# Splitting operations of an attention and feed-forward kernel in two, with a new order list

## The chip, the cores and the metric

The kernel runs on one core of one Trainium2 chip. The metric is the device time of one execution in microseconds. Where the text says TensorE, VectorE, ScalarE, GpSimdE and SyncE, the profile says PE (with PEld for its weight loads), DVE, ACT, POOL and SP.

## The reference

Inputs are q, k and v of 2 batches, 8 heads, 768 positions and 64 channels, and two pairs of weight matrices (512 x 2048 and 2048 x 512).

```
k_sum = max of k over blocks of 32 positions;  v_sum = mean of v over the same blocks
scores_l = q @ k.T / 8, kept where |i - j| < 16, else -1e9
scores_s = q @ k_sum.T / 8 + log(32)
a = softmax over [scores_l, scores_s];  x = a @ [v, v_sum]        # 1536 tokens x 512 channels
h = x @ w_in1;   x = (h * cos(h)) @ w_out1
h = x @ w_in2;   out = (h * clip(h + 3, 0, 6) / 6) @ w_out2
```

## The kernel before

**Attention** is cut into 12 units of 128 queries and all 8 heads. For a unit the keys are the 96 of a window for each half of the queries and the 24 block maxima, together 120 columns. `front(u)` (line 625) loads the queries, puts the mask into two PSUM banks (`masks`, a matmul, or from unit 7 on `seed`, a copy), adds the scores (`scores`), takes the row maxima (`largest`, line 694), the exponentials with their sums (`power`, line 703, one activation for each head), the inverse of the sums, and multiplies with it (`scaled`, line 714). The index j in these operations is the half of the heads, one PSUM bank each. Units 0 and 1 are cut into two groups by heads in another way (`halves`) and so have two of each of these operations already. `back(u)` (line 717) transposes the result on TensorE (`flip`, twice) into bank b, copies it out (`flipped`), multiplies it with the window's values and block means (`weighted`, in 64 small matmuls) and splits the sum into two fp32r parts (`x hi`, `x lo`). The block means of v come from matmuls (`means`, line 580) and are copied by `put_v` (line 589) into rows 96 to 119 of a tile `vcats`: for buffer 0 from PSUM (`put v`, four copies), for buffer 1 from buffer 0 (`put v on`, one copy). This is done once for each batch, so twice.

**Feed-forward.** The weights are loaded, taken apart and put together again as fp32 (`carry`, `rebias`, `shift`, `join`) and split into high and low parts (`hi`, `lo`). Three fp32r products stand for one fp32 product. `first` is the first layer's products (two matmuls in each operation), `turns`, `rest`, `cosine` and `gate` its activation, `second` the second layer's products. In the first stage feed-forward works on 256 tokens at a time, that is on two units, and is woven into the attention of later units; later it works on 512 tokens, in part by block products (`mm1_set`).

**The order.** Every operation is one call of `G.op`, which gives it a number, the engines that may run it and what it reads and writes. Nothing is scheduled by the program: the string `ORDER` (line 39) has one word for each operation, in the order of issue, as `p20+1` or `a1`. The letter is the engine (p TensorE, a ScalarE, v VectorE, g GpSimdE, s SyncE), the number is the operation, and each engine runs its own words in this order, waiting for what they read. `+n` has `fill(n)` (line 1043) issue n matmuls of zeros, 128x512, behind the operation. Ahead of the first feed-forward operation they write into bank d1, which holds nothing yet. Line 1047 is theirs. A word `we` or `ws` loads a table on ScalarE ahead of its use. Loads are issued by SyncE alone, in the order of its words.

The functions that the diff touches:

Of the kernel before, what the change touches and what calls it, by code (L numbers as in the profile page):

```python
# [22 lines left out]
P = 128  # L23
WIN = 16
BLK = 32
# [7 lines left out]
def wstart(w, seq):  # L33
# [6 lines left out]
    s8 p6 s7 s19 s10 s36 a1 g2 s11 v13 a4 a5 s62 s9 v12 p20+1 v0 p21 p37+1 v22 s277 p38+1 v15 a23 s64 v16 a24 v39 p68+2  # L40
    s284 v40 v14 s63 a41 p28+1 v17 p29 v25 s53 a279 v26 v278 p45 g27 a3 v30 p46 a103 s291 v31 p76+2 v47 a32 s84 v280 v48
    s65 p69 v120 p70 a286 v281 p54+2 a49 v33 v287 v42 p55 s66 v34 g35 s67 a77 g282 p85 v56 s101 a293 p78 g283 s80 p86
    v79 a57 s97 a58 v43 v18 v294 p71+3 v292 v50 v87 g295 p72+1 v51 p73 s118 g44 a88 v74 p102 a89 s305 g52 p104 g296 p93
    v59 p81 v60 v105 g61 p95+4 a82 s114 v94 s138 a106 v96 g75 s136 p110+2 v83 v285 p98 v90 v111 g288 s135 v91 p112 a99
    v297 p119 a307 p359 v113 p360 a306 p361 v107 v308 p121 s131 a289 v108 g309 v100 p115 s137 v122 g92 a310 p362 s145
    a116 v142 p347 p348 a123 p363 p349 v117 s298 g311 p371 p364 v140 p350 p127 p372 g109 v128 p351 p352 p373 v139 p129
    a353 s179 p374 a130 p375 v124 g290 v354 p376 a365 v125 p132 a377 v141 s158 g147 v366 p146 s175 v133 g143 a355 p148
    v134 a367 v356 a300 p154 v378 g357 v368 p383 a155 g126 p384 v149 p385 a379 p399 p156 a299 p400 v157 p401 s312 p386
    g358 p402 s188 p159 v301 s162 v380 g302 a150 s189 p403 s190 v160 p404 p417 p418 g303 v161 p387 p419 g369 p395 v304
    p171 s191 g181 a405 p420 v172 p421 a163 p388 s193 p422 g164 v406 p173 s192 a314 p397 g144 v174 p398 g381 a389 p412  # L50
    v151 a423 v315 p176 v313 v152 v390 g153 p165 v177 s223 a407 s206 a391 v178 p396 s319 p411 g316 s210 v166 p413 p194
    p195 p196 p197 v392 g317 p198 we a167 v424 p199 v408 g370 p435 p436 v200 p451 g393 s227 p437 p452 g382 p438 p439
    g318 p440 p415 p453 a441 s326 v180 p414 p416 g212 p202 p429 v442 g394 p182 v203 a425 a443 v409 v426 p204 s244 v183
    g427 p454 p455 g229 p431 p432 v205 g410 we a184 p469 p470 v168 p207 v434 v169 g170 p449 v208 p471 p450 v209 p464
    a211 p466 p430 v320 g201 p219 v444 a321 p456 v220 p213 a433 g428 s333 a328 s240 v322 p221 a457 v214 g323 p472 a222
    p447 p473 a327 p224 v185 v445 a215 v186 s340 v329 g187 v458 p474 v225 s257 p448 p463 p465 v226 p467 p481 g324 p236
    a475 g330 v228 p487 a237 p488 p489 p490 p238 v216 g446 v476 p482 v217 v239 g325 p230 a459 v485 a477 p241 g246 v231
    g218 p468 s265 v242 p491 we a232 p492 p499 v478 p483 v243 p484 g479 v460 p500 p253 v461 p503 v254 p504 p515 p517
    a245 v233 p505 v234 p255 v480 g235 p521 a493 p247 a256 a486 p258 a335 v248 g331 a342 g462 p522 s273 a259 v494 p506
    g332 p507 a249 p501 v260 p519 p502 v336 p516 v334 p261 p518 g337 s556 v262 p533 p523 p524 p263 v250 p508 v251 v264  # L60
# [183 lines left out]
def attention_two_ffn(  # L244
# [344 lines left out]
    def put_v(b, i):  # L589
        mb = "b" if b else "e"  # L590
        every = [("vcs", i, c) for c in range(P // BLK)]
        if i == 0:
            CC = DM // (P // BLK)

            def put(e):
                for c in range(P // BLK):
                    hs = slice(c * CC // D, (c + 1) * CC // D)
                    copy(e, vcat[0][WK:KC, :, hs, :], bank[mb][BLK * c:BLK * c + NB, 0:CC].rearrange(
# [772 lines left out]
```

## Time and profile before

| | us |
|---|---|
| median of 3 runs | 568.65 (568.09 to 569.66) |
| time of the profiled execution | 568.47 |
| its span, first to last instruction | 566.7 |
| TensorE busy | 560.5 |
| VectorE busy | 462.1 |
| ScalarE busy | 340.1 |
| GpSimdE busy | 226.4 |

The profiled execution is one run with the profiler on; its span leaves out what lies around the first and last instruction. A matmul's start is measured and its end modelled, and matmuls overlap in the array, so for TensorE the distance from one start to the next tells more than the duration of one.

### The profile page before, as it was taken

To read this page: it belongs to the slowest core of one execution; us is meant where nothing else is said; L and a number is where in the kernel's file an instruction comes from. 1 tells how busy PE (TensorE), PEld (TensorE's weight loads), DVE (VectorE), ACT (ScalarE), POOL (GpSimd) and SP (SyncE) were. 2 spreads that over 40 slices of the span, in tenths; PEclk is the share of its full clock that TensorE was granted. 3 is DMA by queue.
4 is the path that set the end of the run, shared out by engine and by line. 5 is a ranking of instruction groups with operands and counts; after the bars stand their busy time and mean duration, and the time that the engine had idled before them with its cause. 6 is when DMAs were issued, how large, how long until landed. Compare 5 with 4: busy or idle time off the path is not lost.

```text
span 566.7 us, 9919 instructions
## 1 busy us (share of the span) xinstructions
PE 560.5 (99%) x3741; PEld 478.2 (84%) x3741; DVE 462.1 (82%) x857; ACT 340.1 (60%) x726; POOL 226.4 (40%) x222
## 2 busy tenths in 40 slices
PE   9999999999999999999999999999999999999996
PEld 6789999888888888888889888888888889888885
DVE  6898979888989988979899998777878597766653
ACT  5989995757547786666658677645653443322130
POOL 3788875646533214435253552041132303122111
PEclk9999999999999999999999999999999999999999
DMA  8989532323012211232200222223213220200103
GB/s 318 274 249 294 167 96 99 113 84 102 0 39 74 76 38 38 80 124 95 74 2 1 75 74 75 75 93 132 74 30 119 75 75 1 75 1 1 43 33 149
DMA packets 17232, 51.49 MB, mean 91 GB/s; under 512 B 1952, under 2 KB 2464, under 8 KB 17184
## 3 DMA queue, kind: packets, MB, share of 16 engines
q1 hardware_dynamic: 17184, 50.86, 27.2%
q8 instruction: 29, 0.48, 0.3%
q14 instruction: 19, 0.16, 0.1%
HBM read 47.71 MB, written 3.15 MB: 90 GB/s over the span
## 4 chain that ended last, share of the span: by engine, by line
PE 95%; DMA 2%; POOL 1%; SPq 1%; issue 0%; DVE 0%; ACT 0%; DVEq 0%; POOLq 0%
PE bank_a L1077 24%; PE bank_d L894 16%; PE bank_b L1077 11%; PE bank_c L1077 11%; PE bank_e L894 9%; PE bank_c L894 9%; PE bank_d L946 4%; PE bank_e L946 2%; PE bank_c L946 1%; PE bank_b L736 1%; DMA total<-in_vw_dram 1%; PE bank_b L752 1%; PE bank_c L668 1%; PE bank_d L1047 1%; DMA vcats<-in_vw_dram 1%; PE bank_d L530 1%
## 5 line engine op out<-in xcount | busy, mean ns | idle before, releaser
L517 ACT ACTIVATE cv_t<-raw 128x512 f32<-128x512 f32 x64 | 42.9, 677 | 20.4 <-DVE plo L463 7.5
L522 POOL TENSOR_TENSOR cv_y<-cv_t,cv_y 128x512 int32<-128x512 int32 x25 | 34.4, 1381 | 39.7 <-ACT cv_y L508 18.9
L446 ACT CAST ghi<-hs 128x512 fp32r<-128x512 f32 x43 | 26.5, 617 | 21.6 <-DVE hs L1033 12.8
L1037 DVE TENSOR_TENSOR glo<-hs,ghi 128x512 fp32r<-128x512 f32 x46 | 34.8, 759 | 3.4 <-ACT ghi L446 2.6
L508 ACT ACTIVATE cv_y<-raw 128x512 int32<-128x512 uint32 x47 | 30.9, 668 | 8.5 <-POOL plo L463 4.2
L1037 POOL TENSOR_TENSOR glo<-ch_c,ghi 128x512 fp32r<-128x512 f32 x11 | 15.3, 1390 | 50.7 <-ACT ghi L446 42.4
L520 DVE TENSOR_SCALAR cv_t<-cv_t 128x512 int32<-128x512 int32 x64 | 28.8, 452 | 4.7 <-ACT cv_t L517 4.3
L463 POOL TENSOR_TENSOR plo<-cv_y,phi 128x512 fp32r<-128x512 f32 (+1 forms) x14 | 17.0, 1216 | 32.7 <-ACT phi L446 30.9
L522 DVE CUSTOM_DVE_ANT_0 cv_y<-cv_t,cv_y 128x1024 uint16<-128x1024 uint16 x39 | 27.2, 703 | 1.4 <-ACT cv_y L508 1.3
L714 POOL TENSOR_TENSOR es<-es,rs 128x960 f32<-128x960 f32 (+1 forms) x14 | 21.9, 1565 | 15.5 <-ACT es L706 10.6
L706 ACT ACTIVATE es<-bank_c,nmx 128x120 f32<-128x120 f32 x80 | 27.6, 376 | 0.1
L894 PE MATMUL bank_d<-xhi,plo 128*128 128x256 f32 (+1 forms) x106 | 26.3, 329 | 0.0
L894 PE MATMUL bank_d<-xlo,phi 128*128 128x256 f32 (+1 forms) x106 | 26.2, 329 | 0.0
L894 PE MATMUL bank_d<-xhi,phi 128*128 128x256 f32 (+1 forms) x106 | 26.2, 328 | 0.0
L446 ACT CAST ghi<-ch_c 128x512 fp32r<-128x512 f32 x26 | 16.0, 616 | 12.5 <-DVE ch_c L1033 7.1
L910 DVE TENSOR_TENSOR ch_c<-bank_d,ch_c 128x256 f32<-128x256 f32 (+1 forms) x31 | 14.2, 461 | 10.4 <-PE bank_d L894 8.7
L1124 DVE SCALAR_TENSOR_TENSOR total<-bank_a,total 128x512 f32<-128x512 f32 x28 | 19.0, 685 | 3.3 <-PE bank_a L1077 3.3
L1077 PE MATMUL bank_a<-ghi,whi_out 128*128 128x512 f32 x60 | 21.3, 390 | 0.0
L1077 PE MATMUL bank_a<-ghi,wlo_out 128*128 128x512 f32 x60 | 21.3, 389 | 0.0
L1077 PE MATMUL bank_a<-glo,whi_out 128*128 128x512 f32 x60 | 21.2, 389 | 0.0
L1037 POOL TENSOR_TENSOR glo<-hs,ghi 128x512 fp32r<-128x512 f32 x7 | 10.2, 1457 | 27.5 <-DVE ghi L446 12.5
L894 PEld LDWEIGHTS bank_d<-xhi,phi 128*128 128x128 f32 x106 | 18.8, 189 | 2.8
(398 smaller groups left out, 1967.7 us busy)
## 6 DMA issues: line engine op xcount, KB each, us to landing
raw<-in_w_in_dram SPq DMA_DIRECT2D x32, 512.0 KB, 3.4
raw<-in_w_out_dram SPq DMA_DIRECT2D x32, 512.0 KB, 3.4
vcats<-in_vw_dram SPq DMA_DIRECT2D x12, 384.0 KB, 5.8
qt<-in_q_dram SPq DMA_DIRECT2D x12, 256.0 KB, 6.0
ktile<-in_kt_dram SPq DMA_DIRECT2D x7, 384.0 KB, 5.3
total<-in_vw_dram SPq DMA_DIRECT2D x8, 256.0 KB, 5.3
out_dram<-total SPq DMA_DIRECT2D x8, 256.0 KB, 2.1
vnat<-in_vw_dram SPq DMA_DIRECT2D x4, 256.0 KB, 4.8
```

The costliest lines, as they stand in the source:

```text
L446: nc.scalar.copy(o, i) if e == "ACT" else VEC[e].tensor_copy(o, i)
L508: nc.scalar.activation(y, low.bitcast(U32), AF.Copy, scale=2.0 ** -29)
L517: nc.scalar.activation(o, a, AF.Prelu, scale=2.0 ** -112, alpha=-2.0 ** 32)
L520: G.op("shift", {"DVE": dve(DM, 2)}, lambda e: nc.vector.tensor_scalar(t, t, 3, None, ALU.logical_shift_left), w=[tk], twice=True)
L522: G.op("join", {"POOL": pool(DM), "DVE": dve(DM)}, lambda e: VEC[e].tensor_tensor(y, t, y, ALU.add), r=[tk], w=[yk], twice=True)
L706: nc.scalar.activation(ef[:, j, hp], s4[j][:, hp, :], AF.Exp, bias=nmx[:, j, hp:hp + 1], scale=scale if direct else 1.0, accum_out=sm[:, j ...
L714: G.op("scaled", {"POOL": pool(2 * nz * KC, 1.25) - 0.07, "DVE": dve(2 * nz * KC)}, lambda e, ef=ef, rs=rs, nz=nz: VEC[e].tensor_tensor(ef ...
L894: nc.tensor.matmul(o, wt[i][:, A[a], kk * P:(kk + 1) * P], xt[:, kk, :], start=first and p + kk == 0, stop=p + kk == 3, skip_group_check=True)
L946: nc.tensor.matmul(h, w["in"][i][:, kk * P:(kk + 1) * P], x[blk][:, kk, c0:c1], start=p + kk == 0, stop=p == 2 and kk == NK - 1)
L1037: G.op("g lo", {"DVE": dve(N), "POOL": pool(N)}, lambda e: VEC[e].tensor_tensor(gbuf("lo", s)[:, 0:N], c(), gh().bitcast(F32), ALU.subtrac ...
L1077: nc.tensor.matmul(acc(s, i)[0], l, r, start=first, stop=end and p == 2 and (N == TOK or i % 2 == 1), skip_group_check=N < TOK)
L1124: G.op("sums", {"DVE": dve(TOK)}, lambda e: nc.vector.scalar_tensor_tensor(t(), a, 1.0 / 6.0 if m else 1.0, t(), ALU.mult, ALU.add), r=[ak ...
```

## The change

Four kinds of operation become two operations each, with the same instructions in them except where the text says otherwise:

- `largest` of units 4 to 11 and `power` of units 2 to 11: one operation for each bank j.
- `scaled` of units 2 to 11: one operation on each half of the heads. This was one instruction of 128x960 and is two of 128x480.
- `put v`: two copies in each operation instead of four in one.
- `put v on`: two copies of half the heads instead of one of all.

The keys on which the operations depend are made finer in the same way, so that a transpose of the first half waits for the first half's scaling alone. This adds 32 operations (2,579 to 2,611).

```
-            G.op("put v", {...}, put, r=[mb], w=every)
+            for cs in ((0, 1), (2, 3)):
+                G.op("put v", {...}, lambda e, cs=cs: put(e, cs), r=[mb], w=[every[c] for c in cs])
...
-            G.op("put v on", {...}, ..., r=[("vcs", 0, c) for c in range(P // BLK)], w=every, twice=True)
+            for half in range(2):
+                hs = slice(half * H // 2, (half + 1) * H // 2)
+                G.op("put v on", {...}, ..., r=[("vcs", 0, c) for c in (2 * half, 2 * half + 1)], w=every[2 * half:2 * half + 2], twice=True)
...
+            for js in (both,) if direct else ((0,), (1,)):
+                G.op("largest", {...}, ..., r=[spk[j] for j in js], w=key("max" if direct else "mx", js))
...
+            for js in (both,) if first else ((0,), (1,)):
+                G.op("power", {...}, ..., r=key("mx", js) + [spk[j] for j in js], w=key("e", js) + key("sm", js), table="exp")
...
+            for js in (both,) if first else ((0,), (1,)):
+                G.op("scaled", {...}, ..., r=key("rs", js), w=key("e", js), twice=True)
```

`ORDER` is written anew. From TensorE's word for `first#116` on, at about 100 us, the sequence of every engine is as before; the order ahead of it is changed. TensorE's words up to the first feed-forward operation, with names for numbers (the count behind # is that of the operation of this kind in the program):

```
before: wake masks#0+1 scores#0 masks#2+1 scores#2+1 means#0+2 masks#1+1 scores#1 masks#3 scores#3 flip#0+2 means#1 means#2
        masks#4+2 scores#4 masks#5 flip#1 scores#5 means#3+3 means#4+1 means#5 masks#6 scores#6 flip#2 weighted#0 flip#3+4
        flip#4+2 weighted#1 flip#5 masks#7 first#6
after:  wake masks#0+1 scores#0 masks#2+4 scores#2+2 means#0+1 masks#1 scores#1+3 masks#3 scores#3+2 flip#0+2 masks#4 scores#4
        flip#2 means#1 means#2 masks#5 scores#5 flip#1+6 means#3 means#4+1 means#5 masks#6 scores#6 flip#3+2 weighted#0+3
        flip#4+4 weighted#1 masks#7 flip#5 first#6
```

The zero matmuls in them are 20 before and 31 after. Between the first feed-forward operation and the last weighted sum stand 124 operations `first` and `second` before and 114 after; the rest follow it.

74 operations change their engine, all in this part. The larger groups: `flipped` 8 from VectorE to ScalarE and 4 back; `x hi` 4 from ScalarE to VectorE; `carry` 4 to ScalarE and 3 to VectorE; `join` and `lo` 8 from GpSimdE to VectorE and 4 back; `g hi` and `g lo` 6 from GpSimdE to VectorE and 5 back; `hi` 3 from ScalarE to GpSimdE; `seed` 2 from ScalarE to VectorE and 1 back; for the second batch half of `put v` from VectorE to ScalarE and half of `put v on` from GpSimdE to VectorE; `scaled` of one group of unit 0 and one half of the last unit from GpSimdE to VectorE.

GpSimdE's order has the first half of `put v on` ahead of the scaling of unit 2, where the whole stood behind it, and the copies of keys (`window`, `put k`) of units 6 and 7 further ahead. SyncE's order has the queries of unit 2 in the tenth place instead of the 13th and those of unit 5 ahead of the window load of unit 1 instead of behind it; the other loads of keys, values and weights change places with their neighbours. On ScalarE `x hi` of units 0 and 1 is gone from between the exponentials.

## Rows read from the trace of the kernel before

**Rows 1.** The page, its first line and part 1 (busy us, share, instructions).

```profile
span 566.7 us, 9919 instructions
...
PE 560.5 (99%) x3741; PEld 478.2 (84%) x3741; DVE 462.1 (82%) x857; ACT 340.1 (60%) x726; POOL 226.4 (40%) x222
```

**Rows 2.** The timeline of TensorE: start us, us, what, matmuls merged (x).

```profile
29.04 0.64 PE L946 MATMUL bank_d<-xhi,phi 128*128 128x256 f32 x4
29.52 0.40 PE L946 MATMUL bank_d<-xhi,plo 128*128 128x256 f32 x2
...
103.76 0.84 PE L946 MATMUL bank_e<-xhi,plo 128*128 128x512 f32 x3
104.44 1.07 PE L946 MATMUL bank_e<-xlo,phi 128*128 128x512 f32 x4
```

**Rows 3.** The table of windows; its second line names the columns.

```profile
core 0: us, PE busy (x) PEld busy (x) DVE busy (x) ACT busy (x) POOL busy (x), PEclk, DMA share, GB/s
1.05:29.04 27.99, 27.99 (x471) 20.63 (x472) 21.20 (x56) 21.22 (x97) 15.63 (x32) 1.00 0.95 306
29.04:98.00 68.96, 68.38 (x971) 63.23 (x971) 60.56 (x125) 60.53 (x183) 52.52 (x54) 1.00 0.58 183
...
40.00:60.00 20.00, 19.79 (x291) 18.29 (x290) 17.19 (x37) 19.06 (x55) 17.05 (x22) 1.00 0.76 251
60.00:80.00 20.00, 20.00 (x314) 18.64 (x314) 16.44 (x38) 19.57 (x69) 15.91 (x15) 1.00 0.42 121
```

**Rows 4.** The table of waits of TensorE, whole run.

```profile
PE bank_d L530 <- DVE zero L378: 1.1, 1, 1.1
PE bank_c L668 <- POOL kcat L623: 0.4, 1, 0.4
PE bank_b L582 <- DMA total<-in_vw_dram: 0.2, 1, 0.2
```

**Rows 5.** Groups of the first 100 us by line and shape: count | busy us, mean ns.

```profile
L714 POOL TENSOR_TENSOR es<-es,rs 128x960 f32<-128x960 f32 x10 | 17.9, 1793 | 5.8 <-DVE rs L713 4.9 <-ACT es L706 0.9
...
L1047 PE MATMUL bank_d<-zero 128*128 128x512 f32 x20 | 7.3, 439 | 0.0
...
L446 ACT COPY pts<-bank_b 120x512 f32<-120x512 f32 x8 | 4.8, 600 | 1.0 <-PE bank_b L736 0.9
...
L714 POOL TENSOR_TENSOR es<-es,rs 128x480 f32<-128x480 f32 x4 | 3.9, 996 | 9.7 <-ACT es L706 9.7
...
L446 POOL COPY vcats<-vcats 24x1024 f32<-24x1024 f32 x2 | 2.3, 1166 | 0.1
...
L446 DVE COPY vcats<-bank_b 24x256 f32<-24x256 f32 x4 | 1.7, 423 | 0.4 <-PE bank_b L582 0.4
```

**Rows 6.** The timeline of TensorE around three groups of zero matmuls.

```profile
6.50 0.39 PE L1047 MATMUL bank_d<-zero 128*128 128x512 f32 x1
6.82 0.56 PE L670 MATMUL bank_c<-ktile,qt 64*64 64x96 f32 x16
...
20.77 0.49 PE L1047 MATMUL bank_d<-zero 128*128 128x512 f32 x1
21.20 0.43 PE L582 MATMUL bank_e<-total,avg 128*32 128x128 f32 x8
...
25.02 1.18 PE L1047 MATMUL bank_d<-zero 128*128 128x512 f32 x4
26.04 0.60 PE L736 MATMUL bank_b<-ident,es 128*120 128x128 f32 x4
```

**Rows 7.** The timeline of TensorE around two masks.

```profile
16.92 0.48 PE L644 MATMUL bank_a<-mask_hi,twice 64*128 64x480 f32 x2
17.33 0.65 PE L736 MATMUL bank_d<-ident,es 128*120 128x128 f32 x4
...
37.72 0.70 PE L644 MATMUL bank_c<-mask_hi,eighth 128*128 128x480 f32 x2
38.80 1.05 PE L668 MATMUL bank_c<-kcat,qt 64*64 64x120 f32 x32 [0.37 <-POOL kcat L623]
```

More of the change, by code (lines that the diff above doesn't have):

```diff
@@ L39 @@
 ORDER = """
[L40 to L59, printed above, removed]
@@ L593, in put_v, with put @@
             CC = DM // (P // BLK)
-            def put(e):
-                for c in range(P // BLK):
+            def put(e, cs):
+                for c in cs:
                     hs = slice(c * CC // D, (c + 1) * CC // D)
@@ L599, in put @@
                         "n (h d) -> n h d", d=D).unsqueeze(1).to_broadcast([NB, 2, CC // D, D]))
-            G.op("put v", {"ACT": 4 * act(2 * CC) + 0.2, "DVE": 4 * dve(2 * CC) + 0.3}, put, r=[mb], w=every)
-        else:
-            G.op("put v on", {"POOL": one(2 * DM), "DVE": dve(2 * DM, 2), "ACT": act(2 * DM)}, lambda e: copy(
-                e, vcat[i][WK:KC].rearrange("n a h d -> n (a h d)"), vcat[0][WK:KC].rearrange("n a h d -> n (a h d)")),
-                r=[("vcs", 0, c) for c in range(P // BLK)], w=every, twice=True)
+            for cs in ((0, 1), (2, 3)):
+                G.op("put v", {"ACT": 2 * act(2 * CC) + 0.1, "DVE": 2 * dve(2 * CC) + 0.15}, lambda e, cs=cs: put(e, cs),
+                     r=[mb], w=[every[c] for c in cs])
+        else:
+            for half in range(2):
+                hs = slice(half * H // 2, (half + 1) * H // 2)
+                G.op("put v on", {"POOL": one(DM), "DVE": dve(DM, 2), "ACT": act(DM)}, lambda e, hs=hs: copy(
+                    e, vcat[i][WK:KC, :, hs].rearrange("n a h d -> n a (h d)"), vcat[0][WK:KC, :, hs].rearrange("n a h d -> n a (h d)")),
+                    r=[("vcs", 0, c) for c in (2 * half, 2 * half + 1)], w=every[2 * half:2 * half + 2], twice=True)
     BESIDE, DIRECT, SEEDED = (1, 3), 4, 7
@@ L701, in front, with power @@
                      r=key("max"), w=key("mx"), twice=True)
-            def power(e, ef=ef, s4=s4, nmx=nmx, sm=sm, nz=nz):
-                for j in range(2):
+            def power(e, js, ef=ef, s4=s4, nmx=nmx, sm=sm, nz=nz):
+                for j in js:
                     for hp in range(nz):
@@ L720, in back @@
         ef = es[ei].rearrange("p j h c -> p (j h) c")
-        ek = [("e", ei, 0), ("e", ei, 1)]
+        ek = [[("e", ei, *((x, j) if u < 2 else (j, x))) for x in range(2)] for j in range(2)]
         pt = pts[pi]
```

259 lines of the change are left out of this document (142 added, 117 removed).

## The prediction, before the run

> **What bounds the kernel now.** The page is read first, for the busy shares: TensorE is busy 99% of the 566.7 us span, and no other engine reaches 85% [rows 1]. A busy TensorE is not yet one at its limit, so the next view is the timeline of TensorE late in the run. There three matmuls of 512 columns start within 0.68 us, 0.227 us each, with nothing between them, and at 29 us four of 256 columns within 0.48 us, 0.12 us each [rows 2]; 512 columns at 2.4 GHz would be 0.213 us. So from about 98 us to the last matmul at 562 us TensorE runs at a steady rate that no other engine holds back.
>
> The Trainium skill ("Perfetto Trace Analysis", Identifying the Most-Contended Engine) says that matmul busy time flatters TensorE and that the weight loads' busy share shows the headroom better. Its share here is 84% [rows 1], which would leave room; the steady 0.227 us says that this room isn't open to an order list. What follows if it were is the second rival.
>
> Everything that the new order list moves lies ahead of that steady stretch, so the third view is the table of windows [rows 3]. From 1.05 us, where TensorE begins, to 29.04 us, where the first feed-forward matmul starts, it is busy throughout; from there to 98 us it is busy 68.38 of 68.96 us. The granted clock is at full speed in both. The table of waits gives three rows for the whole run, 1.1, 0.4 and 0.2 us [rows 4], and the 1.1 us is the wait before the very first matmul. TensorE is thus never idle for long even in the first stage. That is not because attention fills it: 20 zero matmuls of line 1047 are among its work there [rows 5]. They stand in the order list as "+n" and run whether something is late or not.
>
> This gives the rule by which I add up: **the end is what TensorE has to execute plus its waits**. A shorter chain on VectorE, ScalarE or GpSimdE pays only if TensorE has a wait to lose, or if zero matmuls leave the list.
>
> **The change, part by part.** *Zero matmuls.* The old list has 20 in 11 groups, the new one 31 in 12, all ahead of the first feed-forward operation. Price of one, from start to next start [rows 6]: the group of four takes 26.04 - 25.02 = 1.02 us, a single one 6.82 - 6.50 = 0.32 us, so each further one in a group is (1.02 - 0.32)/3 = 0.23 us and opening a group adds 0.09 us. 11 more in one more group: 11 x 0.23 + 0.09 = 2.6 us. Upper bound: the mean of their durations, 0.44 us [rows 5], gives 11 x 0.44 = 4.8 us. I take 2.6, because durations overlap in a pipeline and starts don't, and most of the new ones stand inside groups of three to six.
>
> *Other TensorE work.* Masks, scores, transposes, means and weighted sums are the same operations. The same ones stand ahead of the first feed-forward operation in both lists (8 masks, 7 scores, 6 means, 6 groups of transposes, 2 weighted sums). After it, the list of before breaks off feed-forward for attention 28 times, the new one 29 times. Cost 0.
>
> *Waits that can go.* In the old trace I find these by comparing like with like. Of five single zero matmuls two took 0.32 to 0.33 us; one at 20.77 us took 0.43 us [rows 6], and two more as long as that: 0.33 us too much together. The masks at 37.72 us took 1.08 us to the next start where those at 16.92 us took 0.41 us, and the scores behind them waited for GpSimdE's copy of keys [rows 7, 4]: 0.67 us. The means of the second batch waited 0.2 us for a load [rows 4]. Together 1.2 us. The first two groups should go: TensorE reaches its start-up work later behind the extra zero matmuls, and the new list has the keys' copies earlier in GpSimdE's order and a feed-forward operation between those masks and their scores. The load stays. So 1.0 us goes, out of bounds of 0 and 1.2.
>
> *The split operations.* Maxima are two reductions and exponentials eight activations per unit already; each operation is only cut between its instructions. Cost 0 in work, and the second half no longer waits for the first. Scaling becomes two instructions: 128x960 on GpSimdE takes 1.79 us and 128x480 1.00 us [rows 5], so 0.2 us more for each of 10 units, 2.0 us on GpSimdE. TensorE's other work hides it; with that cover gone it would cost at most 2.0. The copies from PSUM into V's block rows are four of 0.42 us before and after [rows 5]; for the second batch two of them move from VectorE to ScalarE, 0.84 us. The copy from one buffer to the other takes 1.17 us [rows 5] and becomes two; each half lies between 0.58 us (time by length) and 1.17 (time by instruction), and I take the lower, as scaling's halves did nearly that, so nothing is added; the upper end is 1.17 us on GpSimdE, hidden like the scaling. Its first half now stands ahead of a scaling, where the whole stood behind one, so what waits for it can start up to 0.6 us sooner. What waits is TensorE's second weighted sum, and seven zero matmuls stand between it and the first weighted sum in the new list, six in the old: the gain is spent there.
>
> *Moved loads and queues.* SyncE's list has the third unit's queries three places earlier and the sixth's ahead of the second window load. Transfers stream at 306 GB/s up to 29 us [rows 3], so what is moved forward moves something else back: the second window by one query load of 262 KB, 0.9 us. TensorE asks for that window over a microsecond later than before, by the zero matmuls ahead of it. Cost 0, or 0.9 us if that cover is gone. GpSimdE issues no transfers.
>
> *Sum.* 2.6 - 1.0 = 1.6 us over the profiled execution's 568.47 us would be 570.1 us. That execution lies 0.18 us under the median of the runs, 568.65, which have a spread of 1.6 us; measured from the median the step would reach 570.25. I predict 570.0, a little under the sum, because small waits of 0.1 us that I couldn't single out can go too. About 0.3%, or 1.7 us, is what a measurement of this kernel can tell from no change, so the forecast is "no change", close to the edge of slower.
>
> **The rivals.** *Slower, because ScalarE falls behind from 40 to 80 us.* There it is busy 19.06 and 19.57 of 20 us [rows 3]: 1.37 us is free. The new list wants attention done ten feed-forward operations earlier (114 instead of 124 stand ahead of the last weighted sum), each two matmuls of 0.12 us: 2.4 us earlier relative to TensorE's work, and 0.8 us earlier on the clock after 1.6 us of delay. In these windows it also gives ScalarE one transposed copy more at 0.60 us, a weights' cast of as many columns, and two block copies at 0.42 [rows 5], and takes away a carry and the two parts of a seed, three operations of about those 0.60 us: 0.2 us more. So 1.0 us must be found in 1.37. If all of it can be used, TensorE waits for nothing; with half, 0.3 us; with none, 1.0 us. It would wait at transposes for the copies out of bank b, with feed-forward work queued behind in order. Above 0.3 us these waits carry the forecast over the edge: +1.9 to +2.6 us, 570.7 us in the middle. For it: ScalarE's shares, the highest of any engine but TensorE there. Against it: ScalarE has idle time before 40 us too, and in the old list TensorE waited for it nowhere [rows 4].
>
> *Faster, because the zero matmuls are free.* If TensorE's busy rows hide waits, then the 31 zero matmuls only stand where it would have waited, and the shorter chains show: all 1.2 us of waits and the 0.6 us of the halved copy go, -1.8 us, 566.7 us. Against it: between 6.5 and 29 us the next start comes after each kind of operation at the same distance nearly everywhere, so there is no hidden slack to spend. The rule of the Trainium skill cited above ("Perfetto Trace Analysis", Identifying the Most-Contended Engine) would favour this case; the trace agrees only in that the weight loads aren't full.
>
> *Even, because every wait goes.* 2.6 - 1.2 and the 0.6 us of the halved copy: +0.8 us, 569.3 us.
>
> **How the numbers follow.** Forecast 0.36, even 0.16, ScalarE late 0.30, faster 0.08, and 0.10 for zero matmuls nearer to their upper price or waits elsewhere. The first two are within 0.3%, 0.52; ScalarE and the last make slower 0.40. The predicted time is the forecast's, 570.0. The range goes from 568.6 (the even case less 0.7, half the spread of the runs) to 572.2 (the ScalarE case's upper end, 571.1, with zero matmuls at 0.33 us instead of 0.23, another 1.1); it leaves out the faster case and the tails.
>
> **What would show it.** In the changed profile, 31 zero matmuls, and the first feed-forward matmul at about 29.04 + 2.6 - 0.3 = 31.3 us. If it starts before 29.0, the sum over TensorE's work is wrong and the faster rival holds. If TensorE's waits name ScalarE between 40 and 80 us, or its busy time between the first feed-forward matmul and the last weighted sum falls short by a microsecond, the ScalarE rival holds. The steady stretch should be unchanged: 0.227 us a matmul, the same order. If it is not, the argument that the change ends at about 100 us is wrong.

## The result and the profile after

The changed kernel takes 573.7 us (median of 6 runs, 572.97 to 574.52) against 568.4 us for the kernel before (568.09 to 569.66): a ratio of 1.0091, 95% interval 1.0078 to 1.0104, so slower by 0.9%. The forecast was 570.0 us, "no change", with a range up to 572.2. The profiled execution took 573.49 us, 5.02 us more than the one of before; all differences in this section are between these two executions. Ratios leave disturbed runs out, medians do not.

The page, its first line and part 1 (busy us, share, instructions), to be held against [rows 1]:

```profile
span 571.7 us, 9957 instructions
...
PE 564.0 (99%) x3752; PEld 480.3 (84%) x3752; DVE 469.3 (82%) x859; ACT 341.9 (60%) x730; POOL 223.2 (39%) x229
```

The eleven further TensorE instructions are the eleven zero matmuls. VectorE is busy 7.2 us longer for two instructions more. Counted by kind and shape at the mean durations of before, the exchange of instructions between engines explains about a quarter of its added instruction time; the rest is the same kinds of instruction taking longer. The windows, for [rows 3], with the first one cut at the new start of feed-forward work, 30.85 us:

```profile
core 0: us, PE busy (x) PEld busy (x) DVE busy (x) ACT busy (x) POOL busy (x), PEclk, DMA share, GB/s
1.05:30.85 29.80, 29.80 (x483) 21.95 (x483) 20.91 (x53) 22.36 (x99) 17.53 (x35) 1.00 0.89 289
30.85:98.00 67.15, 65.32 (x948) 60.20 (x947) 62.65 (x128) 60.49 (x183) 47.66 (x57) 1.00 0.56 181
40.00:60.00 20.00, 19.14 (x304) 17.18 (x302) 18.98 (x38) 18.45 (x54) 16.44 (x19) 1.00 0.72 248
60.00:80.00 20.00, 19.23 (x274) 17.75 (x269) 18.90 (x39) 18.56 (x64) 15.72 (x20) 1.00 0.41 130
```

Ahead of feed-forward work TensorE is busy throughout, as before, only 1.81 us longer. Behind it it is idle for 1.83 us up to 98 us where it was idle for 0.58. From 40 to 80 us ScalarE is busy less than before and VectorE more: 18.98 and 18.90 us instead of 17.19 and 16.44. The waits of TensorE over the whole run, for [rows 4] (us in total, times, longest):

```profile
PE bank_d L532 <- DVE zero L380: 1.1, 1, 1.1
PE bank_e L958 <- DVE ch_e L1040: 0.8, 1, 0.8
PE bank_b L764 <- DVE pts L448: 0.7, 1, 0.7
PE bank_d L958 <- DVE ch_c L1040: 0.5, 1, 0.5
PE bank_e L906 <- DVE ch_c L922: 0.2, 1, 0.2
PE bank_b L764 <- DMA vcats<-in_vw_dram: 0.2, 1, 0.2
```

Four of the five that come behind the first matmul name VectorE. No row names ScalarE.

**Where the 5 us are.** For each kind of TensorE operation I added up the distances from one start to the next in both traces. The first feed-forward matmul is 1.81 us later: zero matmuls, with the eleven of the wake-up, take 13.96 us instead of 11.25 (+2.71), masks, means and transposes 0.9 us less. Behind it, scores take 8.62 us instead of 6.87 (+1.75, the waits behind them for copies included), the step to the products at 46.30 us +0.87, at 121.97 us +0.62, at 304.69 us +0.40, the wait for a window load at 38 us +0.27; masks and means together save 0.95. That is 1.81 + 1.75 + 0.87 + 0.62 + 0.40 + 0.27 - 0.95 = 4.77 of the 5.02 us. The wait of 0.7 us for `pts` in the table of waits, at 75.44 us, lies behind scores and is part of the 1.75. So a third of the loss lies ahead of feed-forward work, and the rest at a handful of single places behind it.

**What VectorE does at those places.** The timeline of the changed kernel around three of them (start us, us, engine, line, operation):

```profile
44.18 1.17 DVE L448 CAST ghe<-ch_e 128x256 fp32r<-128x256 f32 x1
45.27 0.65 DVE L702 TENSOR_REDUCE nmx<-bank_c 128x4 f32<-128x480 f32 x1
45.84 0.41 DVE L1040 TENSOR_TENSOR ch_e<-bank_e,ch_e 128x256 f32<-128x256 f32 x1
...
43.92 1.28 POOL L524 TENSOR_TENSOR cv_y<-cv_t,cv_y 128x512 int32<-128x512 int32 x1
...
46.30 0.51 PE L958 MATMUL bank_e<-xhi,phi 128*128 128x256 f32 x2 [0.80 <-DVE ch_e L1040]
...
56.93 0.98 DVE L720 TENSOR_SCALAR sme<-sm 128x8 f32<-128x8 f32 x1
...
56.90 0.98 POOL L726 TENSOR_TENSOR es<-es,rs 128x480 f32<-128x480 f32 x1
...
58.61 1.52 PE L674 MATMUL bank_c<-kcat,qt 64*64 64x120 f32 x32
...
73.89 0.90 DVE L720 TENSOR_SCALAR sme<-sm 128x8 f32<-128x8 f32 x1
...
73.31 1.46 POOL L524 TENSOR_TENSOR cv_y<-cv_t,cv_y 128x512 int32<-128x512 int32 x1
...
75.44 0.74 PE L764 MATMUL bank_b<-pts,vcats 120*64 120x64 f32 x18 [0.67 <-DVE pts L448]
```

An addition over 128x8 elements, which usually takes 0.17 us, takes 0.98 and 0.90 us. Each began while a GpSimdE instruction was running and ended as that one did (56.93 + 0.98 = 57.91 beside 57.88; 73.89 + 0.90 = 74.79 beside 74.77). The cast at 44.18 us ended 0.15 us after the join, which ended at 45.20. Behind the addition at 56.93 us the seeds of the next unit came late and stretched the scores to 1.52 us (1.05 is usual); behind the one at 73.89 us the copy that the weighted sum needs; behind the cast the gate that the next products need. The Trainium skill ("SBUF — State Buffer", Who interferes with whom) says that VectorE and GpSimdE have one pair of ports in common, that copies, casts and operations with a constant can want it, and that whichever starts first keeps it for its whole instruction. The trace agrees, with the ends just named.

### The profile page after: what moved, and what is told of

Read it like the earlier page. It is cut to its first block, busy times and chain, and to the rows that moved or that the text cites. A ratio compares the mean times of both kernels' runs of the same rounds, so it can differ in the third digit from the quotient of the medians.

```text
span 571.7 us, 9957 instructions
## 1 busy us (share of the span) xinstructions
PE 564.0 (99%) x3752; PEld 480.3 (84%) x3752; DVE 469.3 (82%) x859; ACT 341.9 (60%) x730; POOL 223.2 (39%) x229
## 4 chain that ended last, share of the span: by engine, by line
PE 92%; DVE 5%; DMA 1%; ACT 0%; issue 0%; DVEq 0%; ACTq 0%
PE bank_a L1089 23%; PE bank_d L906 15%; PE bank_c L1089 10%; PE bank_b L1089 10%; PE bank_e L906 9%; PE bank_c L906 8%; PE bank_d L958 4%; PE bank_e L958 2%; PE bank_b L764 2%; PE bank_d L1059 2%; DMA vcats<-in_vw_dram 1%; PE bank_b L748 1%; PE bank_c L958 1%; PE bank_c L674 1%; PE bank_d L532 1%; DVE total L1136 1%
## 5 line engine op out<-in xcount | busy, mean ns | idle before, releaser
L524 POOL TENSOR_TENSOR cv_y<-cv_t,cv_y 128x512 int32<-128x512 int32 x22 | 30.7, 1399 | 34.8 <-ACT cv_y L510 18.9
L1049 POOL TENSOR_TENSOR glo<-ch_c,ghi 128x512 fp32r<-128x512 f32 x12 | 16.8, 1403 | 50.4 <-ACT ghi L448 42.1
L524 DVE CUSTOM_DVE_ANT_0 cv_y<-cv_t,cv_y 128x1024 uint16<-128x1024 uint16 x42 | 30.4, 730 | 1.2 <-ACT cv_y L510 1.1
L465 POOL TENSOR_TENSOR plo<-cv_y,phi 128x512 fp32r<-128x512 f32 (+1 forms) x12 | 14.1, 1174 | 32.3 <-ACT phi L448 32.2
L726 POOL TENSOR_TENSOR es<-es,rs 128x480 f32<-128x480 f32 x22 | 21.9, 1008 | 10.3 <-DVE rs L722 7.0
L1089 PE MATMUL bank_a<-wlo_out,ghi 128*128 128x512 f32 x60 | 21.0, 390 | 0.0
```

The costliest lines, as they stand in the source:

```text
L524: G.op("join", {"POOL": pool(DM), "DVE": dve(DM)}, lambda e: VEC[e].tensor_tensor(y, t, y, ALU.add), r=[tk], w=[yk], twice=True)
L726: :, js[0]:js[-1] + 1], nz=nz, n=n: VEC[e].tensor_tensor(
L1049: G.op("g lo", {"DVE": dve(N), "POOL": pool(N)}, lambda e: VEC[e].tensor_tensor(gbuf("lo", s)[:, 0:N], c(), gh().bitcast(F32), ALU.subtrac ...
L1089: nc.tensor.matmul(acc(s, i)[0], l, r, start=first, stop=end and p == 2 and (N == TOK or i % 2 == 1), skip_group_check=N < TOK)
```

## The experiments

All were timed in five rounds against the kernel before, on several chips, and the runs of before beside them have medians of 568.56 to 569.24 us; so it is the ratio that compares rows. The ratios of gate_first, new_old_loads and the two half lists are the least sure, as before itself took 567.88 to 575.04 us beside them. "First product" is the start of the first feed-forward matmul in the profile of that kernel.

| kernel | us | ratio to before, 95% | first product, us |
|---|---|---|---|
| before | 568.4 | 1 | 29.04 |
| after | 573.7 | 1.0091 (1.0078 to 1.0104) | 30.85 |
| split_only | 569.92 | 1.0024 (1.0001 to 1.0048) | 29.38 |
| old_start_new_rest | 572.53 | 1.0052 (1.0024 to 1.0080) | 29.41 |
| new_start_old_rest | 571.13 | 1.0018 (0.9994 to 1.0042) | 31.34 |
| new_no_sums | 572.42 | 1.0067 (1.0054 to 1.0080) | 30.85 |
| sum_reduce | 572.7 | 1.0069 (1.0055 to 1.0083) | 30.90 |
| gate_first | 573.95 | 1.0074 (1.0048 to 1.0099) | 31.05 |
| new_no_zeros | 572.33 | 1.0059 (1.0047 to 1.0072) | 31.02 |
| old_no_zeros | 568.4 | 1.0002 (0.9987 to 1.0016) | 28.13 |
| new_old_loads | 577.53 | 1.0112 (1.0067 to 1.0157) | 34.47 |
| v_first | 573.48 | 1.0089 (1.0076 to 1.0103) | 30.86 |
| carry_early | 573.97 | 1.0095 (1.0082 to 1.0109) | 31.87 |
| v_first_no_zeros | 571.8 | 1.0047 (1.0027 to 1.0068) | 30.61 |
| after_three | 572.02 | 1.0066 (1.0053 to 1.0078) | 32.02 |
| after_four | 570.27 | 1.0028 (1.0007 to 1.0050) | 29.48 |
| after_four_21 | 571.17 | 1.0047 (1.0027 to 1.0067) | 28.68 |
| before_11_zeros | 568.39 | 1.0012 (0.9991 to 1.0032) | 29.07 |

### Code or order, start or rest

**split_only** has the code of after with the order of before, the words of a split operation side by side.

```
 functions as in after
-ORDER of after
+ORDER of before, "v36" of a split operation written as its two halves in a row
```

> The split operations in the order of before: each split operation's two words stand side by side where the one stood, on the same engine, and the zero matmuls are the old 20. Theory (the loss lies in the order list): 568.0 to 569.5 us, GpSimdE 2.0 us busier, TensorE's waits the old three. Rival (the splits themselves cost, by two instructions for one on GpSimdE): 570 us or more, with waits for scaling.

It took 569.92 us, 0.4 us over the theory's range and just under the rival's 570; its profiled execution took 568.92 against 568.47. The splitting by itself costs 0.45 us in the trace, 1.3 us in the medians (568.63 for before beside it), and by the ratio's interval anything from nothing to 2.7 us. GpSimdE is busy 1.1 us longer, not the 2.0 expected. Most of the loss comes with the order list.

**old_start_new_rest** and **new_start_old_rest** cut the list at the first feed-forward operation.

```
 functions as in after
-ORDER of after
+words of before up to first#6, then the other words in the order of after
```

> The code of after. Every word that stands in the list of before ahead of the first feed-forward matmul comes first, in that order, on those engines and with its 20 zero matmuls; the rest follows in the order of after. Theory (two separate losses: about 1.8 us ahead of the first feed-forward matmul, about 3.2 us behind it, where VectorE's instructions are held up by GpSimdE's): the first feed-forward matmul starts at about 29.0 us and the time falls by 1.8 us, to about 571.9 us. Rival (one loss: the late start makes what follows late): the time falls to about 568.8 us. Rival (the start costs nothing in the end, because TensorE waits for the same later work anyway): 573.5 us.

```
 functions as in after
-ORDER of after
+words of after up to first#6, then the other words in the order of before
```

> The mirror image: the words of after up to its first feed-forward matmul, 31 zero matmuls among them, then the rest in the order of before. Theory (two separate losses): first feed-forward matmul at about 30.9 us, time about 568.6 + 1.8 = 570.4 us. Rival (one loss that begins with the start): about 573.5 us. Rival (the start costs nothing in the end): 568.7 us.

Measured: 572.53 and 571.13 us, profiled 572.33 and 571.27. From the first product to the last matmul the traces show 536.6 us with the new rest (536.3 in after) and 533.6 with the old one (532.7 in before). The waits of TensorE in the second kernel, over the whole run:

```profile
PE bank_d L532 <- DVE zero L380: 1.1, 1, 1.1
PE bank_c L674 <- POOL kcat L629: 0.8, 1, 0.8
PE bank_b L748 <- POOL es L726: 0.3, 1, 0.3
```

With the old rest no wait names VectorE after the first, though the start is the late one. So the traces show two separate losses, as the theory said, and both rivals fall: a late start does not make what follows late by more than 0.9 us, and a late start is not absorbed. The times alone show less: both lie 0.6 to 0.7 us over the forecasts of 571.9 and 570.4, and the ratio of the second does not tell it from before.

### Behind the start: single instructions of VectorE

**new_no_sums** leaves out the addition of 1e-9 to the row sums; the inverse reads the sums themselves.

```
-            G.op("sum", ..., lambda e, ...: nc.vector.tensor_scalar(sme, sm, 1.0e-9, None, ALU.add), ...)
-            G.op("inverse", ..., lambda e, ...: nc.vector.reciprocal(rs, sme), ...)
+            G.op("sum", ..., lambda e: None, ...)
+            G.op("inverse", ..., lambda e, ...: nc.vector.reciprocal(rs, sm), ...)
```

> The changed kernel without the operation that adds 1e-9 to the sums of exponentials (14 small VectorE instructions; the inverse reads the sums themselves, so that addition is left out). In the profile of the changed kernel two of these take 0.98 and 0.90 us instead of 0.16, each ending with the GpSimdE instruction that began before it, and TensorE's waits at 58.8, 59.9 and 74.5 us, 1.6 us together, follow. Theory (VectorE held up by GpSimdE): 1.0 to 2.0 us less, 571.7 to 572.7 us. Rival (VectorE simply has too much to do, these are two of many): 14 x 0.17 us less work on it and at most 0.5 us less time, 573.2 to 573.7 us.

572.42 us, 1.3 us less; scores behind the first product take 7.09 us instead of 8.62. That leaves open whether the additions were held up or whether an instruction less was enough. **sum_reduce** keeps them and the order, and makes them another form: a reduction over pairs.

```
+    pairs = ring(kv, "sm", 2, [P, H, 2])
+    for x in pairs:
+        nc.vector.memset(x[:, :, 1], 1.0e-9)
...
-            ... nc.vector.tensor_scalar(sme, sm, 1.0e-9, None, ALU.add) ...
+            ... nc.vector.tensor_reduce(sme, sm2, AX.X, ALU.add) ...
```

> After, complete, but the operation sum is another form of instruction on VectorE: a reduction over pairs (sum, 1e-9) instead of an addition of a constant. Reductions stand nowhere among the VectorE instructions that were stretched beside a GpSimdE instruction. Same order, same number of instructions. Theory (the short additions are held up by GpSimdE's instructions): the sums of 0.98 us at 56.93 us and 0.90 us at 73.89 us take 0.2 us, TensorE's wait of 0.7 us at 75.4 us goes, time 572.2 to 572.6 us, as without the additions. Rival (it was the instruction less on VectorE that helped, or the sums wait for ScalarE's sums): 573.5 us.

The view of one line gives the shortest, the median and the longest of the 14 instructions in ns, for before, after and this kernel:

```profile
L711 DVE TENSOR_SCALAR sme<-sm x14: 156/163/493, 11.2 to 84.2; 128x8 f32<-128x8 f32 x10, 128x4 f32<-128x4 f32 x4
```

```profile
L720 DVE TENSOR_SCALAR sme<-sm x14: 139/167/978, 10.6 to 88.3; 128x8 f32<-128x8 f32 x10, 128x4 f32<-128x4 f32 x4
```

```profile
L725 DVE TENSOR_REDUCE sme<-sm x14: 131/158/170, 10.6 to 87.7; 128x8 f32<-128x16 f32 x10, 128x4 f32<-128x8 f32 x4
```

The medians are alike. The longest falls from 978 to 170 ns though twice as many elements are read and the order is the same. At the second of the two places the same GpSimdE instruction runs beside it again, and the reduction ends in the middle of it; the weighted sum no longer waits:

```profile
73.50 1.45 POOL L527 TENSOR_TENSOR cv_y<-cv_t,cv_y 128x512 int32<-128x512 int32 x1
...
74.08 0.15 DVE L725 TENSOR_REDUCE sme<-sm 128x8 f32<-128x16 f32 x1
...
74.88 1.15 PE L769 MATMUL bank_b<-pts,vcats 120*64 120x64 f32 x32
```

(At the first place a stall of TensorE, told of below, had moved the sum beside another GpSimdE instruction; it took 0.17 us.) So it was the form of the instruction, beside GpSimdE, that cost the time, and not the work or the place in the list. The whole is 1.0 us faster than after, 0.1 us over the range of 572.2 to 572.6. The Trainium skill ("SBUF — State Buffer", Who interferes with whom) says that reductions never contend for those ports on this chip; the 170 ns agree. In the kernel before the longest is 493 ns, and it too ended as a GpSimdE instruction did:

```profile
69.76 1.29 POOL L522 TENSOR_TENSOR cv_y<-cv_t,cv_y 128x512 int32<-128x512 int32 x1
...
70.59 0.49 DVE L711 TENSOR_SCALAR sme<-sm 128x8 f32<-128x8 f32 x1
```

Such hold-ups were there already, but TensorE's waits named VectorE nowhere behind the first matmul [rows 4].

**gate_first** moves one word.

```
-  p434 v389 s209 g334 v162 p174 a163 s212 v412
+  p434 s209 g334 v162 p174 a163 s212 v412 v389
```

(v389 is the cast g hi#0, v412 gate#2.)

> After, with one word moved: on VectorE the cast g hi#0, which took 1.17 us at 44.18 us beside a GpSimdE join, stands behind gate#2 instead of ahead of it. Theory (an instruction of VectorE held up by GpSimdE delays the gate that TensorE waits for): TensorE's wait of 0.8 us at 46.30 us goes, time about 572.9 us, less what the later places then do. Rival (VectorE is simply late there, whatever stands ahead of the gate): the wait stays over 0.5 us, time 573.5 us or more.

```profile
44.66 0.42 DVE L1040 TENSOR_TENSOR ch_e<-bank_e,ch_e 128x256 f32<-128x256 f32 x1
44.99 0.57 DVE L448 CAST ghe<-ch_e 128x256 fp32r<-128x256 f32 x1
...
45.35 0.50 PE L958 MATMUL bank_e<-xhi,phi 128*128 128x256 f32 x2
...
57.10 1.29 PE L584 MATMUL bank_b<-total,avg 128*32 128x128 f32 x21 [2.06 <-issue]
```

The gate comes 1.18 us earlier and the wait of 0.8 us is gone, as the theory has it. The time did not show it: 573.95 us in the median, at a ratio whose interval takes in the 1.0091 of after. The profiled execution, the slowest of the twelve, took 576.12 us, with a stall of 2.06 us for which the profile names nothing, at the means of the second batch. So the mechanism at that place is shown in the trace and its worth is not shown in the time by this run. In after_three and after_four the wait is gone as well.

The waits at 121.97 and 304.69 us stayed in every kernel with the new rest. At 119.53 us a cast took 1.19 us on VectorE beside a GpSimdE instruction from 119.15 to 120.44, and the gate behind it came late. The order there is that of before, where the same cast began 0.03 us ahead of the GpSimdE instruction and took 0.41 us. Why the product at 304.69 us waits was not followed; split_only, with the order of before, waits 0.2 us at that place too, so it does not take the new order. No edit of those two places was tried.

### The start: zero matmuls and a late load

**new_no_zeros** and **old_no_zeros** leave out all zero matmuls except the eleven of the wake.

```
-            if zeros:
+            if zeros and ZEROS:
...
+ZEROS = False
```

> The changed kernel without its 31 zero matmuls. Theory (TensorE's sum): the new list spends 2.7 us more than the old one on zero matmuls that no wait asks for, so the time falls by far more than 2.7 us if most of them are uncovered; with 42 starts of zero matmuls including the wake-up costing 13.96 us in the profile, 9.1 us belong to the 31, and at least 4 us of it should come off: 565 to 570 us. Rival (they stand where TensorE would wait): waits of the same length take their place, 573 to 574 us. Second rival: without them TensorE falls to its lower clock between 6 and 30 us, and the time is as before or longer, with operations there at twice their distance.

> The kernel before without its 20 zero matmuls (6.4 us from start to next start). Theory (TensorE's sum): some 3 us or more come off, 563 to 566 us. Rival (they stand where TensorE would wait): 568 to 569 us. If the old list loses less than the new one by about 2.7 us, the extra 11 of the new list were uncovered work.

The start of the changed kernel did not come forward, 31.02 us; its time is 1.4 us less all the same, between the theory's range and the rival's (the wait of 0.8 us for the gate is absent from its trace). The start of before came 0.9 us earlier, 28.13, and its time did not change by anything that can be measured. Its profile is that of the fastest of twelve executions, at full clock. Over the twelve the time goes with the granted clock: 567.16 to 568.00 us at a mean of 0.996 or more, 568.80 to 570.85 us at 0.994 or less. The waits of TensorE in new_no_zeros show what came up in place of the zero matmuls:

```profile
PE bank_e L586 <- DMA total<-in_vw_dram: 2.3, 1, 2.3
...
PE bank_e L766 <- DVE xlo L783: 0.9, 1, 0.9
```

Its windows, with the columns as above:

```profile
1.05:22.00 20.95, 17.14 (x331) 12.67 (x331) 14.77 (x39) 15.80 (x70) 11.18 (x28) 1.00 0.94 325
22.00:28.00 6.00, 5.67 (x82) 4.22 (x82) 4.49 (x9) 2.95 (x16) 4.28 (x5) 0.72 0.53 143
```

TensorE waits 2.3 us for a load of v, and from there the granted clock is 0.72 in the mean of six microseconds, so in part at 1.2 instead of 2.4 GHz. Why the load is late shows in the timeline of after, SyncE's and VectorE's lines:

```profile
11.89 0.33 SPq L635 DMA_DIRECT2D qt<-in_q_dram  x1
15.18 0.33 SPq L501 DMA_DIRECT2D raw<-in_w_in_dram  x1
15.55 1.02 SPq L573 DMA_DIRECT2D total<-in_vw_dram  x2
...
14.68 0.42 DVE L512 TENSOR_SCALAR cv_y<-raw 128x512 int32<-128x512 uint32 x1
```

and in its windows:

```profile
15.00:16.00 1.00, 1.00 (x23) 0.59 (x25) 1.00 (x5) 1.00 (x5) 0.49 (x1) 1.00 0.11 43
```

A weights load waits for a buffer that VectorE's carry#0 frees; the carry starts at 14.68 us where it started at 11.46 before, because five operations that stood behind it now stand ahead of it in VectorE's order. Two loads of v queue behind that weights load, and from 15 to 16 us the DMA engines are busy 11% of the time.

**new_old_loads** gives SyncE's first 23 loads the old order.

```
-  s8 s7 s19 s9 s36 s10 s64 s11 s309 s53 s316 s68 s66 s65 s88 s323 s67 s69 ...
+  s8 s7 s19 s10 s36 s11 s64 s9 s309 s66 s316 s65 s53 s323 s88 s67 s68 s69 ...
```

> After, with SyncE's first 23 loads in the order of before; nothing else is moved. Theory (the last means of the start-up wait for a load that the new order of loads makes late, and the zero matmuls stand in that wait): the last means start about 1.5 us earlier than 22.7 us, the first feed-forward matmul at 29.4 to 30.0 us instead of 30.85, time 572.3 to 573.0 us. Rival (VectorE's and ScalarE's new order sets the start, not the loads): first feed-forward matmul at 30.8 us, 573.7 us.

It was worse than either forecast, 577.53 us, first product at 34.47. TensorE waited 1.5 us for maxima of keys: VectorE takes them in the new order, and the loads of keys now came in the old one. The edit moved more than the disputed load, so it says nothing about it; it does show that the two orders belong together.

**v_first** moves only the two loads of v, **carry_early** only the carry.

```
-  s88 s323 s67 s69
+  s67 s69 s88 s323
```

> After, with two words moved on SyncE: the fourth and the sixth load of v stand ahead of the fourth load of queries and the third load of weights, which hold SyncE's queue until 15.2 us while the DMA engines run dry from about 14.5 to 16.4 us. Theory (the start is late because the last load of v is queued behind a weights load that waits for a buffer): the last means start at 21.2 us or earlier instead of 22.7, the first feed-forward matmul at 29.0 to 29.6 us instead of 30.85, time 572.0 to 572.6 us. Rival (VectorE's order sets the start, the load is only one of several things that are late): first feed-forward matmul at 30.5 to 30.9 us, 573.5 us.

```
-  v30 v26 v42 v43 v47 v48 v310 v312
+  v310 v30 v26 v42 v43 v47 v48 v312
```

> After, with one word moved on VectorE: carry#0, which frees the weights' buffer that SyncE waits for, stands ahead of largest#1, where it stood in the list of before, instead of five instructions further on. Loads keep the order of after. Theory (SyncE's queue is held by VectorE's late carry): SyncE's third weights load goes out at about 12.4 instead of 15.2 us, the last means start at about 21 us, the first feed-forward matmul at 29.2 to 29.8 us, time 572.0 to 572.8 us. Rival (as in the run with the loads of v moved): no change, 573.5 us.

Both loads went out at 9.1 and 12.9 us instead of 15.55, and the start did not gain: 30.86 and 31.87 us (in the second a stall of 0.63 us at the means that the profile puts down to nothing). TensorE's operations followed each other at the same distances as in after, zero matmuls included. The times are those of the rivals, but not for the rivals' reason, as the later runs show: neither the load alone nor the zero matmuls alone set the start. In after the last load of v lands at about 22.0 us and the means that read it start at 22.67; in new_no_zeros they start at 22.01. So fewer zero matmuls without an earlier load could bring these means forward by 0.7 us at the most.

**v_first_no_zeros** does both, and **after_four_21** has both with fewer zero matmuls (below).

```
 ORDER of v_first
-  every "+n"
```

> After with the fourth and sixth load of v early on SyncE (as in the run that did only this) and without the zero matmuls (as in the run that did only this). Each edit alone left the first feed-forward matmul where it was, at 30.86 and 31.02 us. Theory (two covers of the same 2.7 us lie beside each other, what TensorE has to execute and the late load, and the start comes forward only when both go): first feed-forward matmul at 28.2 to 29.4 us, time 571.3 to 572.3 us. Rival (a third chain, VectorE's and ScalarE's order for the first two units, stands at the same place): 30.3 us or later, time 572.3 us or more.

30.61 us for the first product where the theory had 28.2 to 29.4: by its number the rival's case. The time, 571.8 us, is in the theory's range. The profile is that of the slowest of the twelve executions, 574.12 us, so it does not stand for them all. The windows of this kernel and of after_four_21, which has the zero matmuls in part, show another reason than a third chain:

```profile
1.00:31.00 30.00, 26.64 (x453) 20.53 (x453) 21.53 (x53) 22.24 (x100) 17.20 (x35) 0.83 0.83 275
```

```profile
1.05:28.68 27.63, 27.29 (x472) 19.91 (x473) 20.38 (x53) 21.69 (x99) 16.84 (x35) 1.00 0.93 302
```

Without zero matmuls TensorE waits in many places (the longest wait, 1.37 us, is for queries and ends at 8.78 us) and the granted clock falls to 0.83 in the mean, and to 0.50 from 10 to 18 us; with 21 of them it stays at full speed and the first product starts at 28.68 us, 2.17 us ahead of after. That a third chain binds when there are none is not excluded. Ten zero matmuls fewer took 11.66 us instead of 13.96: 0.23 us each.

**before_11_zeros** asks the same of the kernel before.

```
-  "+2", "+3", "+4"
+  "+1"
```

> The kernel before with one zero matmul in each of its 11 groups instead of 20 in all; nothing else. Theory (TensorE's list is what bounds the start in the kernel before too, 0.23 us for each further zero matmul of a group, down to where the waits begin that the run without zero matmuls showed at 28.13 us): first feed-forward matmul at 28.1 to 28.3 us instead of 29.04, clock at full speed, time 567.6 to 568.2 us, the first version that is faster than before. Rival (the gain at the start is lost behind it): 568.4 us or more, and the waits behind 29 us grow by as much.

First product at 29.07 us where 28.1 to 28.3 was expected, time 568.39: nothing gained, at the start or behind it. The zero matmuls took 1.41 us less and the masks 1.29 us more. In that order the further zero matmuls of a group were a cover, in the new order with early loads they were a price.

### The sum

**after_three** has the early carry, gate#2 first and the sums as reductions; **after_four** the early loads of v instead of the early carry, and no zero matmuls; **after_four_21** the same with at most two zero matmuls in a group.

```
 ORDER of after
-  v30 v26 v42 v43 v47 v48 v310
+  v310 v30 v26 v42 v43 v47 v48
...
+  gate_first, sum_reduce
```

> After with three edits at once: carry#0 early on VectorE, the cast g hi#0 behind gate#2, and the sums as reductions. Theory (separate losses that add up: 1.3 us from the start, 0.8 us from the gate, 1.3 us from the sums): time 573.6 - 3.4 = 570.2 us, 570.0 to 571.0. Rival (what is gained at one place is lost at the next, since VectorE is the engine that sets the pace): 572.0 us or more.

```
 ORDER of after
-  s88 s323 s67 s69
+  s67 s69 s88 s323
...
+  gate_first, sum_reduce, no "+n"
```

> After with four edits: the two loads of v early, no zero matmuls, the cast g hi#0 behind gate#2, the sums as reductions. Theory (separate losses that add up): 1.5 to 2.5 us from the start, 0.8 us from the gate and 1.3 us from the sums come off 573.6, so 569.0 to 570.0 us. Rival (the gain at the start is lost behind it, since the later units are late for another reason): 571.3 us or more.

```
 after_four
-  no "+n"
+  "+3", "+4", "+6" as "+2"
```

> The same four edits, but with 21 zero matmuls, at most two in a group, instead of none. Theory (what stands in TensorE's list is executed, 0.23 us for each further zero matmul of a group, and the load no longer covers it): first feed-forward matmul about 1.0 to 2.0 us later than without zero matmuls and about 2.3 us ahead of 30.85 at the earliest; time 569.5 to 571.0 us. Rival (zero matmuls cost nothing, they stand where TensorE would wait): the same time as without them.

after_three took 572.02 us, over its range and just in the rival's. But the stretch from the first product to the last matmul fell from 536.3 to 534.3 us, close to the 2.1 us that gate and sums were priced at; it is the start that gave 1.2 us back, with its first product at 32.02 us: means took 0.72 us more there, with a stall among them, and zero matmuls 0.40 us more. after_four took 570.27 us and after_four_21 571.17, a little over their ranges of 569.0 to 570.0 and 569.5 to 571.0. Without zero matmuls the first product came later than with 21, 29.48 against 28.68 us, at a granted clock of 0.94 against 1.00, though the theory had it 1.0 to 2.0 us earlier; yet the time was not longer. Four edits thus take off 3.4 of 5.3 us. What stays is about 1 us at the two places, now at 118 and 302 us, and a stall in both profiles (1.09 us in after_four, 0.78 in after_four_21); the rest was not traced to a place. No version beat the kernel before in the median.

## Why the prediction was wrong

**Zero matmuls: the size was right.** Eleven more cost 2.71 us between starts against 2.6, the first product came at 30.85 us against 31.3, and ten fewer gave 2.30 us back (after_four_21). The rule behind it, that the start is what TensorE has to execute plus its waits, held only as long as nothing else came up underneath. "There is no hidden slack to spend" was wrong: new_no_zeros shows 2.3 us of waiting for a load under the 31 zero matmuls, before_11_zeros a wait of the masks under the old 20. The rival that zero matmuls stand in waits was right in that. It was wrong that the time would fall: where two things cover the same stretch, the start takes the longer of the two.

**The failed step is the sum of waits.** "So 1.0 us goes", and with it nothing comes. Waits did go, 0.87 us ahead of the first product and 0.95 behind it (masks and means), but 3.9 us came: 1.75 + 0.87 + 0.62 + 0.40 + 0.27. The largest term that was to go was not compared like with like: the masks at 37.72 us have 128 rows and those at 16.92 have 64 [rows 7], and the former took 0.54 us in the new order, so 0.54 us went there and not 0.67. New waits had no term in the forecast's sum; the case that came, "waits elsewhere", had a share of the last 0.10 of the chances, and the range left it out. I searched the old trace for waits that the new order would remove and did not ask which instructions of VectorE would fall beside GpSimdE's in the new one. The old trace had the sign of it: an addition of 493 ns in a line whose median is 163. A mean per group hides that.

**The splits at cost 0, "TensorE's other work hides it".** As code they cost 0.45 us in the trace of split_only. But one half of "put v on" for the second batch, moved to VectorE, took 0.95 us beside a scaling, where the other half took 0.61 us on GpSimdE. It stands ahead of the seeds of a unit whose scores then took 1.43 us instead of 1.05:

```profile
63.13 1.93 POOL L726 TENSOR_TENSOR es<-es,rs 128x480 f32<-128x480 f32 x2
...
64.40 0.95 DVE L448 COPY vcats<-vcats 24x512 f32<-24x512 f32 x1
...
67.00 1.43 PE L674 MATMUL bank_c<-kcat,qt 64*64 64x120 f32 x32
```

In sum_reduce the copy still takes 0.95 us and these scores 1.26, so 0.2 us of it can be the copy's; no run moved the copy alone. I counted work and durations of the old engine, and no hold-up.

**The rival "ScalarE falls behind"** was the right kind of loss, new waits from 40 to 80 us, on the wrong engine. It had been chosen by the busy share, 19.06 and 19.57 of 20 us [rows 3]. ScalarE was then busy less and TensorE never waited for it. VectorE had 2.8 and 3.6 us free there [rows 3] and yet it was the one that came late, because what counts is the one late instruction ahead of the one that TensorE needs.

**The moved loads at "Cost 0".** The window load cost 0.27 us, within the bound of 0.9. The step missed that SyncE's list waits for buffers which VectorE frees: carry#0, five instructions later on VectorE, held a weights load, and two loads of v behind it, for some 3 us. The zero matmuls hid it; without them it was the bound, with a wait of 2.3 us (new_no_zeros).

**"The steady stretch should be unchanged."** Its rate is (0.227 us a matmul), and so is its order. It still lost 1.02 us at two places. At the first, a cast of VectorE began behind a GpSimdE instruction instead of just ahead of it; the second was not followed.

## What to carry to other kernels

An order list that leaves the work as a whole alone can still cost most of a per cent, by which instruction of VectorE starts behind one of GpSimdE's; look at the longest instruction of a line beside its median, and at who waits behind it, and put a small operation that sits on such a path into a form that showed no hold-up. When two covers lie beside each other, such as filler matmuls and a late load, taking out either alone shows nothing: take both, and watch the granted clock, since filler that goes may take the clock with it. And when a step is moved back on one engine, ask which buffer it frees and what is queued behind the load that waits for it.

## What the runs showed of the hardware

In seven of the profiles TensorE stalled with no wait that the profile can name: 2.06 us in gate_first, 1.52 in sum_reduce, 1.09 in after_four, 0.78 in after_four_21, 0.72 in new_old_loads, 0.63 in carry_early and 0.32 in after_three, at means of either batch or, in after_four, at the scores behind them. Each stall ended 1.27 to 1.59 us after the end of a 16 KB transfer on the DMA queue that the profile calls "q8 instruction". The sixth of these transfers ended at 51.24 us in after and at 53.27 in new_no_sums, which have no stall at the second batch's means, at 54.42 in sum_reduce, where the stall ended at 55.92, and at 55.52 in gate_first, where it ended at 57.10. So TensorE most likely waited there for its own instructions; from 55 to 57 us in gate_first the DMA engines were busy throughout. This is read from times alone, no run tested it, and why the transfer came later in some executions stays open.

In gate_first the window behind the stall shows the clock that followed:

```profile
58.00:62.00 4.00, 4.00 (x29) 3.55 (x25) 2.76 (x7) 2.04 (x5) 1.27 (x1) 0.65 0.04 15
```

After the pause the granted clock was 0.65 for four microseconds, though TensorE was busy throughout them. After the 1.52 us of sum_reduce it stayed at 1.00. Such stalls may be part of why the times of one kernel differ by a microsecond or two.
